# One token per partition in the q/k loads, a quarter of `w_in` ahead, and constants set later, in a chunk-selected attention with a squared-ReLU MLP

## The chip, the cores and the metric

The kernel runs on one core of one Trainium2 chip. The metric is the device time of an execution, in microseconds (us). The kernel before spread over 337.4 to 341.1 us from run to run, and its median over 338.4 to 339.5 us from call to call, so differences below about 1 us between runs of different calls are not read.

## The reference

Attention over 4 batches, 8 heads, 768 tokens and 64 dimensions, in which each query sees only the 6 key chunks (of 32 keys) with the highest upper bound, followed by an MLP with squared ReLU on all 3072 tokens:

```python
k_chunks = k.reshape(B, H, nc, 32, D)                       # nc = 24 chunks
k_min, k_max = k_chunks.min(3), k_chunks.max(3)
ub = sum_d(max(q * k_min, q * k_max))                       # per query and chunk
ub = where(causal_by_chunk, ub, -1e9)
top_chunks = argsort(ub)[..., -6:]
scores = q @ k.T / sqrt(D), masked to top_chunks and to causal positions
attn = softmax(scores) @ v
x = attn.transpose(0, 2, 1, 3).reshape(3072, 512)
h = maximum(x @ w_in, 0)                                    # 512 -> 2048
out = (h * h) @ w_out                                       # 2048 -> 512
```

## The kernel before

The heads go in pairs, and the 768 tokens of a sequence in two halves ("blocks") of 384. `stage_a` prepares a pair: it transposes k and q on TensorE, forms the chunk minima and maxima, the bounds and the selection. `stage_b` makes the scores, exponentials and weighted values of one pair and block, and writes x transposed (`xT`). When all four pairs of a block are done, its MLP units join a list that later `stage_b` calls work off between their own matmuls. The first block of batch 0 has no finished block's MLP beside it, and only six `w_in` matmuls of its own MLP units run in it: I call it the *first stage*, and its end is the last `xT` of pair 3. Pairs are counted from 0, as in the code.

The loads of batches 0 and 1 put three neighbouring tokens on one partition, 384 B of bf16 in one piece. After the transpose the columns are therefore in a permuted order, and copies restore it:

```python
WIDE = (0, 1)
def load_qk(b, h0, h1, halves=(0, 1), what="kq"):
    ...                                                     # [cut]
        if b not in WIDE:     # "h (j p) d -> p (h j) d": one token per partition
            ...
        elif len(halves) == 2:
            nc.gpsimd.dma_start(
                out=dst[:, h0:h1].rearrange("p h t x -> p (h t) x"),
                in_=src[b, h0:h1].rearrange(
                    "h (t p j) d -> p (h t) (j d)", t=2, j=HT))
        else: ...             # the same for one half
```

```python
# stage_a, for k; pt holds the transposed tile in PSUM
if b in WIDE:
    kt = work.tile([128, QB * nt], BF16, tag="kt", name="kt")
    nc.vector.tensor_copy(kt.rearrange("d (t p j) -> d t p j", t=nt, j=HT), by_token)
    flat = kt
...                           # chunk max and min from flat -> kr
for hh in range(2):
    nc.vector.tensor_copy(kbd[s][rows, :, hh, 12 * n0:12 * n1], kr[rows])
    nc.vector.tensor_copy(kq[s][hh][0:D, cols], flat[rows])
# for q
for hh in range(2):
    if b in WIDE:
        nc.scalar.copy(qs[s][hh]..., by_token[rows])             # permuting, on ACT
        src, dst = qs[s][hh][0:D, u0:u0 + m], rows               # then from SBUF
    else: ...                                                    # straight from PSUM
    nc.vector.tensor_scalar_max(qp[dst, 0:m], src, 0.0)
    nc.vector.tensor_scalar_min(qm[dst, 0:m], src, 0.0)
```

The constants, `w_in` and the order of the pieces:

```python
def set_constants(s):
    nc.vector.memset(kbd[s], 0.0)
    for hh in range(2):
        nc.vector.memset(qs[s][hh][D:KC, 0:128], 0.0)
    nc.vector.memset(selb[s], 0.0)
    ...                                                          # [cut]
set_constants(0)
nc.vector.memset(vo[0][:, :, :, D:], 1.0)     # the ones beside v
set_constants(1)
...                                                              # [cut]
put(0, 1, L(load_qk, 0, 0, H, (1,)), L(load_w_in))   # the whole of w_in, 2 MB
put(0, 2, L(load_v, 0, 1))
...                                                              # [cut]
put(1, 0, L(load_qk, 1, 0, H), L(load_w_out), L(load_v, 1))
phases[0][1:1] = [L(set_constants, 2), L(set_constants, 3)]
for ss in range(NP, NSET):
    put(0, ss % NP, L(set_constants, ss))
put(1, 2, L(nc.vector.memset, vo[1][:, :, :, D:], 1.0))
```

`put(ph, i, x)` puts x into the text of the program ahead of pair i in block `ph` (counted over the batches).

The softmax here doesn't subtract the row's maximum and nothing guards it: scores larger than these inputs give would overflow.

Of the kernel before, what the change touches and what calls it, by code (L numbers as in the profile page):

```python
# [10 lines left out]
BF16 = mybir.dt.bfloat16  # L11
AX = mybir.AxisListType
ALU = mybir.AluOpType
ACT = mybir.ActivationFunctionType
# [4 lines left out]
def kernel(  # L19
# [9 lines left out]
    nc = tc.nc  # L29

    B, H, S, D = q.shape
    CH = 32
# [32 lines left out]
    WIDE = (0, 1)  # L65

    def load_qk(b, h0, h1, halves=(0, 1), what="kq"):


        for nm, src in (("k", k), ("q", q)):  # L70
            if nm not in what:
                continue
            if (nm, b) not in nat:
                nat[nm, b] = ld.tile([128, H, 2, HT * D], BF16, tag=nm + "n",
                                     name=nm + "n")
            dst = nat[nm, b]
            if b not in WIDE:
                nc.gpsimd.dma_start(
                    out=dst[:, h0:h1].rearrange(
                        "p h t (j d) -> p (h t j) d", d=D),  # L80
                    in_=src[b, h0:h1].rearrange(
                        "h (j p) d -> p (h j) d", p=128))
            elif len(halves) == 2:
                nc.gpsimd.dma_start(
                    out=dst[:, h0:h1].rearrange("p h t x -> p (h t) x"),
                    in_=src[b, h0:h1].rearrange(
                        "h (t p j) d -> p (h t) (j d)", t=2, j=HT))
            else:
                t = halves[0]
                nc.gpsimd.dma_start(  # L90
                    out=dst[:, h0:h1, t],
                    in_=src[b, h0:h1, QB * t:QB * t + QB].rearrange(
                        "h (p j) d -> p h (j d)", j=HT))
# [35 lines left out]
    def set_constants(s):  # L129
# [3 lines left out]
        nc.vector.memset(selb[s], 0.0)  # L133
# [10 lines left out]
    nc.vector.memset(vo[0][:, :, :, D:], 1.0)  # L144
    set_constants(1)

# [12 lines left out]
    load_v(0, 0)  # L159
# [4 lines left out]
    def load_w_in():  # L164
        nc.gpsimd.dma_start(
            out=w_in_sb, in_=moe_w_in.rearrange("(ki p) f -> p ki f", p=128))
# [5 lines left out]
    def stage_a(p, halves):  # L172
# [10 lines left out]
        for nm in ("k", "q"):  # L183
            pt = pool.tile([128, nt, HT, 128], BF16, tag=tag, name=nm + "T")
            n = nat[nm, b].rearrange("p h t (j d) -> p h t j d", d=D)
            for t in range(nt):
                for j in range(HT):
                    for hh in range(2):
                        nc.tensor.matmul(  # L189
                            pt[D * hh:D * hh + D, t, j],  # L190
                            lhsT=n[:, 2 * hp + hh, n0 + t, j], rhs=ident,
                            is_transpose=True, start=True, stop=True)
            flat = pt.rearrange("d t j p -> d (t j p)")
            by_token = pt.rearrange("d t j p -> d t p j")
            if nm == "k":
                if b in WIDE:
                    kt = work.tile([128, QB * nt], BF16, tag="kt", name="kt")
                    nc.vector.tensor_copy(  # L198
                        kt.rearrange("d (t p j) -> d t p j", t=nt, j=HT),
                        by_token)  # L200
                    flat = kt
                kr = work.tile([128, 2, NC // 2 * nt], BF16, tag="kr",
                               name="kr")
                for mm, op in ((0, ALU.max), (1, ALU.min)):
                    nc.vector.tensor_reduce(  # L205
                        kr[:, mm], flat.rearrange("d (c j) -> d c j", j=CH),
                        axis=AX.X, op=op)
                for hh in range(2):
                    rows = slice(D * hh, D * hh + D)
                    nc.vector.tensor_copy(  # L210
                        kbd[s][rows, :, hh, 12 * n0:12 * n1], kr[rows])
                    nc.vector.tensor_copy(kq[s][hh][0:D, cols], flat[rows])  # L212
                yield
                continue
            qp = work.tile([128, S], BF16, tag="qp", name="qp")
            qm = work.tile([128, S], BF16, tag="qm", name="qm")
            for hh in range(2):
                rows = slice(D * hh, D * hh + D)
                if b in WIDE:
                    nc.scalar.copy(  # L220
                        qs[s][hh][0:D, cols].rearrange(
                            "d (t p j) -> d t p j", t=nt, j=HT),
                        by_token[rows])
                    src, dst = qs[s][hh][0:D, u0:u0 + m], rows
                else:
                    nc.vector.tensor_copy(qs[s][hh][0:D, cols], flat[rows])  # L226
                    if hh == 0:
                        continue
                    src, dst = flat[:, u0 - QB * n0:], slice(0, 128)
                nc.vector.tensor_scalar_max(qp[dst, 0:m], src, 0.0)  # L230
                nc.vector.tensor_scalar_min(qm[dst, 0:m], src, 0.0)  # L231
# [195 lines left out]
    put(0, 1, L(load_qk, 0, 0, H, (1,)), L(load_w_in))  # L427
# [15 lines left out]
    for ss in range(NP, NSET):  # L443
        put(0, ss % NP, L(set_constants, ss))
    put(1, 2, L(nc.vector.memset, vo[1][:, :, :, D:], 1.0))
# [50 lines left out]
```

## Time and profile before

| | before |
|---|---|
| time, median of 3 runs | 338.78 us (338.65 to 339.1) |
| span of the profile | 337.1 us |
| end of the first stage (last `xT` of pair 3) | 48.4 us |
| TensorE (PE) idle in the whole span | 42 us |

The page's line of busy times, and its line of PE in 40 equal slices (each digit is tenths busy, 9 is 90% or more, a slice is 8.4 us):

```profile
PE 295.1 (88%) x2096; PEld 159.0 (47%) x2096; DVE 219.4 (65%) x678; ACT 227.9 (68%) x562; POOL 90.4 (27%) x226
...
PE   1564759989999799999999999999999999999995
```

PE is the limit from about the seventh slice on. What can be won is its idle time at the start. The table of stretches, cut at the ends of the first stage and of later blocks, gives each engine's busy time in each:

```profile
core 0: us, PE busy (x) PEld busy (x) DVE busy (x) ACT busy (x) POOL busy (x), PEclk, DMA share, GB/s
0.00:48.40 48.40, 23.68 (x147) 11.61 (x148) 37.43 (x137) 20.51 (x48) 25.23 (x52) 1.00 1.16 145
48.40:101.60 53.20, 48.90 (x393) 25.62 (x392) 45.92 (x152) 41.10 (x99) 16.67 (x35) 1.00 1.02 94
101.60:174.80 73.20, 69.30 (x544) 38.38 (x543) 55.67 (x166) 53.47 (x134) 20.57 (x48) 1.00 0.50 50
...
```

In the first stage VectorE (DVE) is the busiest, 37.4 of 48.4 us; PE is busy for half of it. PE's waits in the first 50 us (total, times, longest):

```profile
PE ub L243 <- DVE qp L230: 7.6, 3, 5.2
PE ph L302 <- DMA w_in_sb<-in_moe_w_in_dram: 5.2, 1, 5.2
PE kT L189 <- DMA kn<-in_k_dram: 4.3, 1, 4.3
PE sT L263 <- DVE selb L255: 3.5, 3, 1.7
```

The chain that ended last runs through both large stops (start, length, what):

```profile
2.12 2.62 DVE vo L144
...
19.32 15.74 DMA w_in_sb<-in_moe_w_in_dram
35.11 0.82 PE ph L302 x2
```

So DVE set the ones of `vo[0]` before any key was touched, and PE's queue stood behind the first `w_in` matmul until 35.1 us. DVE's timeline around 30 us shows the second set of ones, of `vo[1]`, right ahead of the step of pair 3's selection that PE waits for (`selb`). It is the fourth selection of the stage; the prediction and three of the expectations call it pair 2's.

```profile
29.99 2.62 DVE L424 MEMSET vo<- 128x3072 bf16 x1 [0.59 <-PE av_507 L359]
32.52 0.20 DVE L255 TENSOR_TENSOR selb<-ubm,m_466 128x96 bf16<-128x96 f32 x1
...
36.18 0.60 DVE L268 COPY qsc<-sT 24x256 bf16<-24x256 bf16 x2 [3.01 <-PE sT L263]
```

Some of the costs of DVE in the first stage, by group (busy us, mean ns):

```profile
L212 DVE COPY kqc<-kt 64x384 bf16<-64x384 bf16 x10 | 4.8, 483 | 0.1
...
L144 DVE MEMSET vo<- 128x3072 bf16 x1 | 2.6, 2618 | 0.6 <-issue 0.6
L424 DVE MEMSET vo<- 128x3072 bf16 x1 | 2.6, 2618 | 0.6 <-PE av_507 L359 0.6
```

A `kqc` copy takes 0.25 us when nothing disturbs it. The timelines of DVE and of GpSimd (POOL) show why one of them took 2.03 us: it lay beside the issue of a DMA by POOL.

```profile
42.84 2.03 DVE L212 COPY kqc<-kt 64x384 bf16<-64x384 bf16 x1
```

```profile
42.57 2.21 POOL L102 DMA_DIRECT2D vo<-in_v_dram  x1
```

### The profile page before, as it was taken

How to read it: one execution, taken by the hardware profiler on the slowest of the kernel's cores; microseconds unless marked ns; L12 is line 12 of the kernel's file. 1: busy time of each engine (PE TensorE's matmuls, PEld its weight loads, DVE VectorE, ACT ScalarE, POOL GpSimd, SP SyncE). 2: the span in 40 equal slices, each digit the busy share in tenths (PEclk: the TensorE clock that was granted, in tenths of full speed). 3: DMA queues.
4: the chain of work that ended last, by engine and by line, in shares of the span. 5: the costliest groups of instructions: out<-in, count | busy, mean ns of one | idle time of the engine just before them, and what ended most of it. 6: DMA issues, size and time to landing. Idle time of an engine off the chain costs nothing.

```text
span 337.1 us, 6126 instructions
## 1 busy us (share of the span) xinstructions
PE 295.1 (88%) x2096; PEld 159.0 (47%) x2096; DVE 219.4 (65%) x678; ACT 227.9 (68%) x562; POOL 90.4 (27%) x226
## 2 busy tenths in 40 slices
PE   1564759989999799999999999999999999999995
PEld 0231324544445454555455555555455555554542
DVE  7988488899889948899177467997384413431420
ACT  3363537989568875877658775888469769983731
POOL 8265431362144430221143221112122212220000
PEclk9999999999999999999999999999999999999999
DMA  7979999799059990000039000000110010001001
GB/s 79 174 106 197 142 188 193 53 94 95 33 63 97 126 91 33 32 2 3 31 50 108 0 33 32 33 2 2 48 48 0 3 62 31 2 0 63 33 31 62
DMA packets 64298, 20.86 MB, mean 62 GB/s; under 512 B 58276, under 2 KB 60684, under 8 KB 64268
## 3 DMA queue, kind: packets, MB, share of 16 engines
q0 software_dynamic: 60272, 13.63, 44.8%
q1 hardware_dynamic: 3996, 6.85, 5.4%
q8 instruction: 16, 0.26, 0.3%
q14 instruction: 14, 0.11, 0.1%
HBM read 27.26 MB, written 6.29 MB: 100 GB/s over the span
## 4 chain that ended last, share of the span: by engine, by line
PE 53%; DVE 29%; ACT 9%; DMA 5%; issue 4%; POOL 1%; ACTq 0%; POOLq 0%
PE py L316 20%; PE ph L302 15%; PE ps L393 6%; DMA w_in_sb<-in_moe_w_in_dram 5%; DVE kr L205 5%; DVE xT L383 4%; ACT rc L373 3%; DVE qp L230 3%; DVE kqc L212 2%; DVE qsc L226 2%; ACT e L397 2%; DVE kt L198 2%; PE sT L263 2%; PE kT L189 2%; DVE qm L231 2%
## 5 line engine op out<-in xcount | busy, mean ns | idle before, releaser
L397 ACT ACTIVATE e<-ps 128x384 bf16<-128x384 f32 (+2 forms) x288 | 111.1, 429 | 35.4 <-PE ps L393 34.0
L302 PE MATMUL ph<-xT,w_in_sb 128*128 128x384 bf16 x512 | 106.9, 330 | 8.9 <-DMA w_in_sb<-in_moe_w_in_dram 5.2
L400 POOL TENSOR_SCALAR_AFFINE_SELECT e<-e 128x128 bf16<-128x128 bf16 x192 | 58.5, 311 | 201.5 <-ACT e L397 199.6
L393 PE MATMUL ps<-qsc,kqc 88*128 88x384 bf16 (+2 forms) x288 | 73.2, 305 | 6.4 <-ACT e L397 4.1
L307 ACT ACTIVATE ht<-ph 128x384 bf16<-128x384 f32 x128 | 63.5, 502 | 16.8 <-PE ph L302 15.8
L302 PEld LDWEIGHTS <-w_in_sb 128*128 128x128 bf16 x512 | 48.5, 98 | 43.0 <-issue 12.2
L393 PEld LDWEIGHTS <-kqc 88*128 88x128 bf16 x288 | 27.5, 100 | 21.9 <-issue 5.4
L359 PEld LDWEIGHTS <-vo 128*128 128x128 bf16 x288 | 27.8, 101 | 19.2 <-issue 2.2
L321 ACT COPY ob<-py 128x512 f32<-128x512 f32 x24 | 14.1, 587 | 19.3 <-PE py L316 19.1
L205 DVE TENSOR_REDUCE kr<-kT 128x24 bf16<-128x768 bf16 x16 | 14.6, 952 | 15.9 <-PE kT L189 15.9
L220 ACT COPY qsc<-qT 64x384 bf16<-64x384 bf16 (+1 forms) x24 | 13.9, 580 | 11.4 <-PE qT L189 11.0
L268 DVE COPY qsc<-sT 24x640 bf16<-24x640 bf16 (+2 forms) x40 | 16.7, 417 | 6.5 <-PE sT L263 5.8
L243 PE MATMUL ub<-kbd,qp 128*128 128x48 bf16 x80 | 8.8, 190 | 11.3 <-DVE qp L230 9.9
L376 ACT ACTIVATE rc<-rc 128x384 f32<-128x384 f32 x32 | 16.5, 515 | 0.1
L205 DVE TENSOR_REDUCE kr<-kt 128x12 bf16<-128x384 bf16 (+1 forms) x24 | 15.5, 677 | 0.2
L189 PE MATMUL kT<-ident,kn 128*64 128x128 bf16 x192 | 11.0, 240 | 4.9 <-DMA kn<-in_k_dram 4.3
L243 PEld LDWEIGHTS <-qp 128*128 128x128 bf16 x80 | 5.8, 98 | 17.2 <-DVE qp L230 13.2
L189 PEld LDWEIGHTS <-kn 128*64 128x64 bf16 x192 | 7.0, 116 | 12.6 <-DMA kn<-in_k_dram 4.3
L263 PE MATMUL sT<-ident,selb 128*128 128x128 bf16 x80 | 8.5, 232 | 4.6 <-DVE selb L255 4.5
L189 PE MATMUL qT<-ident,qn 128*64 128x128 bf16 x192 | 11.0, 240 | 0.9 <-DMA qn<-in_q_dram 0.7
L198 DVE COPY kt<-kT 128x384 bf16<-128x384 bf16 (+1 forms) x12 | 8.3, 691 | 4.7 <-PE kT L189 4.5
L189 PEld LDWEIGHTS <-qn 128*64 128x64 bf16 x192 | 7.1, 117 | 8.6 <-issue 4.7
(653 smaller groups left out, 522.5 us busy)
## 6 DMA issues: line engine op xcount, KB each, us to landing
out_dram<-ob SPq DMA_DIRECT2D x24, 256.0 KB
kn<-in_k_dram POOLq DMA_DIRECT2D x3, 768.0 KB, 9.3
qn<-in_q_dram POOLq DMA_DIRECT2D x3, 768.0 KB, 9.2
vo<-in_v_dram POOLq DMA_DIRECT2D x3, 768.0 KB, 10.2
w_in_sb<-in_moe_w_in_dram POOLq DMA_DIRECT2D x1, 2048.0 KB, 15.7
w_out_sb<-in_moe_w_out_dram POOLq DMA_DIRECT2D x1, 2048.0 KB, 16.1
vo<-in_v_dram POOLq DMA_DIRECT2D x6, 128.0 KB, 8.6
kqc<-kqc SPq DMA_DIRECT2D x15, 36.0 KB
```

Source lines behind the costliest of these rows:

```text
L189: nc.tensor.matmul(pt[D * hh:D * hh + D, t, j], lhsT=n[:, 2 * hp + hh, n0 + t, j], rhs=ident, is_transpose=True, start=True, stop=True)
L205: nc.vector.tensor_reduce(kr[:, mm], flat.rearrange("d (c j) -> d c j", j=CH), axis=AX.X, op=op)
L263: nc.tensor.matmul(sT[:, 128 * i:128 * (i + 1)], lhsT=selb[s][:, u0 - 1 + i:u0 + 1 + i], rhs=ident, is_transpose=True, start=(i == 0), sto ...
L268: nc.vector.tensor_copy(qs[s][hh][D:KC, 128 * u0:128 * t1], sT[32 * hh:32 * hh + NC, :])
L302: nc.tensor.matmul(ph, lhsT=w_in_sb[:, ki, 128 * f:128 * (f + 1)], rhs=xT[:, ki], start=(ki == 0), stop=(ki == NKI - 1))
L307: nc.scalar.activation(ht, ph, ACT.Relu)
L316: nc.tensor.matmul(py, lhsT=h2[f][:, 128 * t:128 * (t + 1)], rhs=w_out_sb[:, f, :], start=(f == 0), stop=(f == NFI - 1))
L359: nc.tensor.matmul(hold["av"][hh][:, off:], lhsT=vo[b % 2].rearrange("p h n d -> p (h n d)")[:, c0:c0 + 2 * D], rhs=es[hh][:, off:], start ...
L376: nc.scalar.activation(rc, rc, ACT.Exp, scale=-1.0)
L393: nc.tensor.matmul(ps[:, off:], lhsT=kq[s][hh][:, 128 * j:128 * (j + 1)], rhs=qs[s][hh][:, q0 + off:q1], start=True, stop=True)
L397: nc.scalar.activation(e[:, off:], ps[:, off:], ACT.Exp, scale=scale)
L400: nc.gpsimd.affine_select(out=e[:, off:off + 128], in_=e[:, off:off + 128], compare_op=ALU.is_ge, fill=0.0, base=0, channel_multiplier=-1, ...
```

## The change

The intent is to shorten the first stage. The change has three parts:

- **Part L, the loads.** Every q/k load puts one token on one partition (packets of 128 B written instead of 384 B). The permuting copies go: k's `kt` copy on DVE and q's copies on ACT. q is copied by DVE, and `kqc`, `qp` and `qm` are made straight from PSUM.
- **Part W, `w_in`.** A quarter of its columns is loaded ahead of the second half of the sequence.
- **Part C, the constants.** The ones of `vo[0]` go to ACT, the zeros of `selb` shrink, and sets 4 to 7 and the ones of `vo[1]` (in six pieces) are written into the program's second block.

```diff
 # part L
-            if b not in WIDE: ...                      # [cut: three forms of load]
+            if j1 - j0 == NT:                          # both halves: one DMA
+                ... src[b, h0:h1].rearrange("h (j p) d -> p (h j) d", p=128)
+            if h1 - h0 <= j1 - j0:                     # few heads: a DMA per head
+                ...
+            for j in range(j0, j1):                    # else a DMA per 128 tokens
+                nc.gpsimd.dma_start(
+                    out=nat[nm, b][:, h0:h1, j],
+                    in_=src[b, h0:h1, 128 * j:128 * (j + 1)].rearrange("h p d -> p h d"))
 # [cut: the transposes, the same matmuls into a plain [128, nt * QB] tile]
+            for hh in range(2):
+                rows = slice(D * hh, D * hh + D)
+                nc.vector.tensor_copy(ops[s][hh][0:D, cols], pt[rows])   # k and q
             if nm == "k":
-                if b in WIDE: kt = ...; nc.vector.tensor_copy(kt..., by_token)
-                    nc.vector.tensor_copy(kq[s][hh][0:D, cols], flat[rows])
-            for hh in range(2): ...                    # [cut: q on ACT; qp, qm by halves]
+        nc.vector.tensor_scalar_max(qp[:, 0:m], pt[:, u0 - QB * n0:], 0.0)
+        nc.vector.tensor_scalar_min(qm[:, 0:m], pt[:, u0 - QB * n0:], 0.0)
 # part W
-    put(0, 1, L(load_qk, 0, 0, H, (1,)), L(load_w_in))
+    load_w_in(0, 4)                                    # after load_v(0, 0)
+    put(0, 1, L(load_qk, 0, 0, H, (1,)), L(load_w_in, 4, NFI))
 # part C
-        nc.vector.memset(selb[s], 0.0)
+        nc.vector.memset(selb[s][:, :, :, NC:], 0.0)
+        nc.vector.memset(selb[s][:, NT - 1], 0.0)
-    nc.vector.memset(vo[0][:, :, :, D:], 1.0)
+    for j in range(2):
+        nc.scalar.activation(vo[0][:, :, HT * j:HT * (j + 1), D:],
+            ident[:, 0:1]...to_broadcast([128, H, HT, D]), ACT.Copy, scale=0.0, bias=1.0)
-        put(0, ss % NP, L(set_constants, ss))
-    put(1, 2, L(nc.vector.memset, vo[1][:, :, :, D:], 1.0))
+        put(1, 1, L(set_constants, ss))
+    for j in range(NT):
+        put(1, j // 2 + 1, L(nc.vector.memset, vo[1][:, :, j, D:], 1.0))
```

More of the change, by code (lines that the diff above doesn't have):

```diff
@@ L63 @@
     nat = {}
-    WIDE = (0, 1)
     def load_qk(b, h0, h1, halves=(0, 1), what="kq"):
@@ L73, in load_qk @@
             if (nm, b) not in nat:
-                nat[nm, b] = ld.tile([128, H, 2, HT * D], BF16, tag=nm + "n",
+                nat[nm, b] = ld.tile([128, H, NT, D], BF16, tag=nm + "n",
                                      name=nm + "n")
-            dst = nat[nm, b]
-            if b not in WIDE:
+            j0, j1 = HT * halves[0], HT * (halves[-1] + 1)
+            if j1 - j0 == NT:
                 nc.gpsimd.dma_start(
-                    out=dst[:, h0:h1].rearrange(
-                        "p h t (j d) -> p (h t j) d", d=D),
-                    in_=src[b, h0:h1].rearrange(
-                        "h (j p) d -> p (h j) d", p=128))
-            elif len(halves) == 2:
-                nc.gpsimd.dma_start(
-                    out=dst[:, h0:h1].rearrange("p h t x -> p (h t) x"),
-                    in_=src[b, h0:h1].rearrange(
-                        "h (t p j) d -> p (h t) (j d)", t=2, j=HT))
-            else:
-                t = halves[0]
-                nc.gpsimd.dma_start(
-                    out=dst[:, h0:h1, t],
-                    in_=src[b, h0:h1, QB * t:QB * t + QB].rearrange(
-                        "h (p j) d -> p h (j d)", j=HT))
+                    out=nat[nm, b][:, h0:h1].rearrange("p h j d -> p (h j) d"),
+                    in_=src[b, h0:h1].rearrange("h (j p) d -> p (h j) d",
+                                                p=128))
+                continue
+            if h1 - h0 <= j1 - j0:
+                for h in range(h0, h1):
+                    nc.gpsimd.dma_start(
+                        out=nat[nm, b][:, h, j0:j1],
+                        in_=src[b, h, 128 * j0:128 * j1].rearrange(
+                            "(j p) d -> p j d", p=128))
+                continue
+            for j in range(j0, j1):
+                nc.gpsimd.dma_start(
+                    out=nat[nm, b][:, h0:h1, j],
+                    in_=src[b, h0:h1, 128 * j:128 * (j + 1)].rearrange(
+                        "h p d -> p h d"))
     vo = [consts.tile([128, H, NT, 2 * D], BF16, tag=f"vo{s}", name="vo")
@@ L143 @@
     set_constants(0)
-    nc.vector.memset(vo[0][:, :, :, D:], 1.0)
     set_constants(1)
+    for j in range(2):
+        nc.scalar.activation(
+            vo[0][:, :, HT * j:HT * (j + 1), D:],
+            ident[:, 0:1].unsqueeze(2).unsqueeze(3).to_broadcast(
+                [128, H, HT, D]), ACT.Copy, scale=0.0, bias=1.0)
     ubmask = consts.tile([128, NS, 1, NC], F32, tag="ubmask")
@@ L158, with load_w_in @@
         )
-    load_v(0, 0)
     w_in_sb = consts.tile([128, NKI, d_ff], BF16, tag="w_in_sb")
     w_out_sb = consts.tile([128, NFI, d_model], BF16, tag="w_out_sb")
-    def load_w_in():
+    def load_w_in(f0, f1):
+        cols = slice(128 * f0, 128 * f1)
         nc.gpsimd.dma_start(
-            out=w_in_sb, in_=moe_w_in.rearrange("(ki p) f -> p ki f", p=128))
+            out=w_in_sb[:, :, cols],
+            in_=moe_w_in[:, cols].rearrange("(ki p) f -> p ki f", p=128))
+    load_v(0, 0)
+    load_w_in(0, 4)
     def load_w_out():
@@ L183, in stage_a @@
         for nm in ("k", "q"):
-            pt = pool.tile([128, nt, HT, 128], BF16, tag=tag, name=nm + "T")
-            n = nat[nm, b].rearrange("p h t (j d) -> p h t j d", d=D)
-            for t in range(nt):
-                for j in range(HT):
-                    for hh in range(2):
-                        nc.tensor.matmul(
-                            pt[D * hh:D * hh + D, t, j],
-                            lhsT=n[:, 2 * hp + hh, n0 + t, j], rhs=ident,
-                            is_transpose=True, start=True, stop=True)
-            flat = pt.rearrange("d t j p -> d (t j p)")
-            by_token = pt.rearrange("d t j p -> d t p j")
-            if nm == "k":
-                if b in WIDE:
-                    kt = work.tile([128, QB * nt], BF16, tag="kt", name="kt")
-                    nc.vector.tensor_copy(
-                        kt.rearrange("d (t p j) -> d t p j", t=nt, j=HT),
-                        by_token)
-                    flat = kt
+            pt = pool.tile([128, nt * QB], BF16, tag=tag, name=nm + "T")
+            for j in range(nt * HT):
+                for hh in range(2):
+                    nc.tensor.matmul(
+                        pt[D * hh:D * hh + D, 128 * j:128 * (j + 1)],
+                        lhsT=nat[nm, b][:, 2 * hp + hh, n0 * HT + j], rhs=ident,
+                        is_transpose=True, start=True, stop=True)
+            ops = kq if nm == "k" else qs
+            for hh in range(2):
+                rows = slice(D * hh, D * hh + D)
+                nc.vector.tensor_copy(ops[s][hh][0:D, cols], pt[rows])
+            if nm == "k":
                 kr = work.tile([128, 2, NC // 2 * nt], BF16, tag="kr",
@@ L205, in stage_a @@
                     nc.vector.tensor_reduce(
-                        kr[:, mm], flat.rearrange("d (c j) -> d c j", j=CH),
+                        kr[:, mm], pt.rearrange("d (c j) -> d c j", j=CH),
                         axis=AX.X, op=op)
@@ L211, in stage_a @@
                         kbd[s][rows, :, hh, 12 * n0:12 * n1], kr[rows])
-                    nc.vector.tensor_copy(kq[s][hh][0:D, cols], flat[rows])
                 yield
-                continue
-            qp = work.tile([128, S], BF16, tag="qp", name="qp")
-            qm = work.tile([128, S], BF16, tag="qm", name="qm")
-            for hh in range(2):
-                rows = slice(D * hh, D * hh + D)
-                if b in WIDE:
-                    nc.scalar.copy(
-                        qs[s][hh][0:D, cols].rearrange(
-                            "d (t p j) -> d t p j", t=nt, j=HT),
-                        by_token[rows])
-                    src, dst = qs[s][hh][0:D, u0:u0 + m], rows
-                else:
-                    nc.vector.tensor_copy(qs[s][hh][0:D, cols], flat[rows])
-                    if hh == 0:
-                        continue
-                    src, dst = flat[:, u0 - QB * n0:], slice(0, 128)
-                nc.vector.tensor_scalar_max(qp[dst, 0:m], src, 0.0)
-                nc.vector.tensor_scalar_min(qm[dst, 0:m], src, 0.0)
+        qp = work.tile([128, S], BF16, tag="qp", name="qp")
+        qm = work.tile([128, S], BF16, tag="qm", name="qm")
+        nc.vector.tensor_scalar_max(qp[:, 0:m], pt[:, u0 - QB * n0:], 0.0)
+        nc.vector.tensor_scalar_min(qm[:, 0:m], pt[:, u0 - QB * n0:], 0.0)
         yield
```

## The prediction

> **What bounds the kernel now.** The page gives PE 295.1 of 337.1 us busy (88%), ACT 68%, DVE 65%. The table of stretches shows where PE's 42 idle us lie: it is busy 25 us of the first 50, 72.7 of 79 us from 49 to 128, and about 96% from 128 to 280. So only the opening, the four head pairs of the first half sequence, has much to give. There the limit is DVE, busy 38.5 of 50 us, with two stops shown by the chain of waits and the timeline:
> - DVE spends 2.62 us (2.12 to 4.74) setting the ones of vo, then about 3 us on other constants, before it touches the first kT at 7.75, though PE had transposed it by 4.8.
> - PE idles from 29.9 to 35.1: pair 2's selection stood behind the second vo memset (2.62 us, until 32.6), and then PE's queue stood behind the first w_in matmul, whose whole-tensor load took 15.7 us to land (5.2 us in the list of waits). Dense matmuls start only at about 49 us. Until then a 384-column matmul takes 0.53 us instead of 0.325.
>
> **What the change does, with durations from the trace.**
> - DVE up to 49 us. Removed: both vo memsets (5.2), five permuting kt copies (0.56 each, 2.8), about 2.5 of memsets of sets 4 to 7, and qp/qm as half-partition pairs (-1.6). Added: eight q copies from PSUM at an estimated 0.35 (as the 24x384 PSUM copies) = 2.8, and 0.1 more for each k copy = 0.8. Net about -8 us. The ones of vo[0] go to ACT, idle then.
> - ACT loses 24 q copies (13.9 us), mostly where it is no limit.
> - PE's wait for w_in goes: a quarter is enough for the first four units and should land at about 20 us.
> - DVE in the second stage (49 to 95): kt copies off (-4.6), q and k copies on (+6.9), qp/qm -1.9, and moved here vo[1] (+3.3) and sets 4 to 7 (+2.5): about +6 us on an engine busy 39 of 46 us. I expect 2 to 3 us back.
> - DMA. The q/k packets of batches 0 and 1 go from 8192 of 384 B written to 24576 of 128 B. The Trainium skill, "DMA: Bandwidth & Descriptors", Specifications, asks for at least 512 B for line rate; the trace agrees mildly: 128 B packets ran at 156 GB/s (70 to 74 us), 1 KB ones at 202 (47 to 52). Half a q/k load costs about 1.5 us more.
> - POOL issues more DMAs (0.77 to 0.9 each): estimated +11 us in the first 50, where it is busy 25. So pair 1's q lands 2 to 3 us later, and selects of e can stand behind issues. The skill's "SBUF — State Buffer", "SBUF: two separate sides", says that DVE and GpSimd can block each other; here a kqc copy took 2.03 us instead of 0.25 during a 2.21 us issue.
>
> **Sum.** First stage ends about 10 us earlier (DVE -8, w_in stop and idle DVE -3, later q +1 to 2), 2 to 3 us returned in the second: net -8. **330.5 us**, range 325 to 336.5. Chances: faster 0.60, same 0.35, slower 0.05.
>
> **What would show it.** First kT-derived DVE work at about 5.5 us; no idle PE of 5 us before the first w_in matmul; dense matmuls from about 39 us; DVE over 90% in the stage after; the last 200 us unchanged.
>
> **What would make it wrong.** The opening bound by POOL's issues or the late q of pair 1 (gain under 4 us); the second stage DVE-bound and returning most of it; the rest of w_in or v's second half landing after its first use.

## The result, and the profile after

| | before | after |
|---|---|---|
| time, median of 4 runs each | 338.94 us (338.65 to 341.06) | 330.22 us (329.88 to 330.36) |
| ratio, after to before | | 0.9728 (95%: 0.9688 to 0.9768) |
| span of the profile | 337.1 us | 328.7 us |
| end of the first stage | 48.4 us | 41.6 us |
| first copy out of a kT by DVE | 7.75 us | 7.97 us |
| first bounds matmul (`ub`) | 11.15 us | 12.08 us |
| first scores matmul (`ps`) | 15.31 us | 16.32 us |
| first `w_in` matmul | 35.11 us | 27.73 us |

Ratios here and below are the mean time of one kernel's runs over the mean of the other's of the same rounds, so they are not quite the ratio of the medians quoted. The first column is the kernel before as run beside the change, so its median is not quite that of the section above. All outputs are right.

The page after, the same two lines (a slice is 8.2 us). 20 matmul records of PE are missing from this trace, as its weight loads still number 2096:

```profile
PE 294.6 (90%) x2076; PEld 158.7 (48%) x2096; DVE 219.1 (67%) x678; ACT 218.2 (66%) x540; POOL 99.1 (30%) x237
...
PE   1397699999998999999999999999999999999995
```

PE's busy time did not change; its idle time went from 42.0 to 34.1 us, and most of that (6.6 us) in the first 50 us, where PE was busy 25.19 us before and 31.83 after. The table of stretches, cut at the same four events (columns as before):

```profile
0.00:41.60 41.60, 23.70 (x144) 11.57 (x145) 34.98 (x138) 18.54 (x40) 34.22 (x62) 1.00 1.44 135
41.60:88.50 46.90, 44.72 (x334) 23.34 (x339) 37.85 (x123) 33.04 (x85) 17.25 (x34) 1.00 1.53 129
88.50:167.50 79.00, 73.50 (x597) 40.32 (x601) 66.42 (x196) 53.89 (x135) 20.12 (x50) 1.00 0.53 51
...
```

Three readings:

1. The first stage is 6.8 us shorter. DVE is busy 2.5 us less in it (37.43 to 34.98) and idle 4.4 us less (48.40 − 37.43 = 11.0, against 41.60 − 34.98 = 6.6). The opening itself gained nothing: the first scores of pairs 0, 1 and 2 began at 15.3, 20.6 and 25.5 us before and at 16.3, 21.5 and 26.5 after. From pair 2's to pair 3's it took 11.0 us before and 5.0 after, which is 6.0 of the gain, and from there to the end of the stage 11.9 and 10.2.
2. The second and third rows can only be compared as a sum, because MLP units moved between them: 126.4 us before, 125.9 after, with 118.2 us of PE work in both. So the second stage gave nothing back that can be seen.
3. The rest, from there to the end of the span, is 1.1 us shorter (162.3 and 161.2 us). The lead over before, measured at each block's last `xT`, is 7.3 us at 167.5 and 7.8 to 8.2 from then on. That last part is at the limit of what the runs resolve.

PE's waits in the first 50 us:

```profile
PE kT L194 <- POOL ident masks.py:199: 4.3, 1, 4.3
PE kT L194 <- DVE kr L206: 3.3, 2, 2.6
```

There is no wait for `w_in` any more. The 4.3 us at the very start is the same wait as before under another name: such a wait is put down to whichever of its releasers came last. The quarter of `w_in` was issued at 14.08 us and landed 8.4 us later, 5 us ahead of the first matmul that reads it:

```profile
27.73 0.52 PE L288 MATMUL ph<-xT,w_in_sb 128*128 128x384 bf16 x1
```

DVE's timeline, at the start and at pair 3's selection:

```profile
5.27 0.48 DVE L410 MEMSET vo<- 128x512 bf16 x1
...
5.85 2.11 DVE L410 MEMSET vo<- 128x512 bf16 x4
7.97 0.72 DVE L201 COPY kqc<-kT 64x384 bf16<-64x384 bf16 x2
...
29.94 0.28 DVE L241 TENSOR_TENSOR selb<-ubm,m_454 128x96 bf16<-128x96 f32 x1
30.99 0.60 DVE L254 COPY qsc<-sT 24x256 bf16<-24x256 bf16 x2 [0.77 <-PE sT L249]
```

Pair 3's selection (the prediction and three of the expectations call it pair 2's) is no longer cut in two, and its result is copied at 30.99 instead of 36.18. But the ones of `vo[1]`, which the source has in the second block, ran at 5.27 to 7.97, ahead of the first work on a key: five of the six pieces there and the sixth at 9.78. The zeros of sets 4 to 7 ran there too. The compiled program had moved both forward. DVE's groups in the first stage that answer to those of before:

```profile
L201 DVE COPY qsc<-qT 64x384 bf16<-64x384 bf16 x10 | 3.5, 353 | 0.2
L201 DVE COPY kqc<-kT 64x384 bf16<-64x384 bf16 x10 | 3.5, 352 | 0.2
L410 DVE MEMSET vo<- 128x512 bf16 x6 | 2.9, 485 | 0.3
```

The `kqc` copy reads PSUM now, which costs 0.35 us instead of the undisturbed 0.25, and yet the group became cheaper: 3.5 instead of 4.8 us. The timelines of DVE and POOL at the long issues show the reason. Only a copy from SBUF (`kbd<-kr`) is stretched; the copies from PSUM, and `qp` and `qm`, ran at their normal length beside two issues:

```profile
35.22 1.78 DVE L211 COPY kbd<-kr 64x24 bf16<-64x24 bf16 x2
...
38.20 0.72 DVE L201 COPY qsc<-qT 64x384 bf16<-64x384 bf16 x2
...
39.21 0.35 DVE L217 TENSOR_SCALAR qm<-qT 128x384 bf16<-128x384 bf16 x1
```

```profile
34.62 2.23 POOL L75 DMA_DIRECT2D kn<-in_k_dram  x1
36.84 2.23 POOL L75 DMA_DIRECT2D qn<-in_q_dram  x1
39.04 1.18 POOL L176 DMA_DIRECT2D w_out_sb<-in_moe_w_out_dram  x1
```

This fits two pages of the Trainium skill taken together. "SBUF — State Buffer", "Who interferes with whom", says that a DVE instruction in a two-port mode and a GpSimd instruction block each other, and that one with at most one SBUF input outside those modes does not. "VectorE: DVE Perf Modes", "Why PSUM operands drop a tier", says that an operand in PSUM rules the two-port mode out. The traces agree in one more respect: over the first 130 us of before, after and all runs below, every DVE operation held for more than 0.4 us beside an issue read SBUF, and ended between 0.04 us before and 0.16 us after the end of the issue (one exception, 0.59 us after, in `late_q_on_act`).

To put a number on it I use one measure throughout, the **collision loss**: for each DVE instruction that lay beside a DMA issue by POOL, its duration above the lower quartile of all instructions of the same line and shapes, where that excess is over 0.1 us, summed over the first 130 us. It was 4.9 us before and 2.9 us after.

### The profile page after: what moved, and what is told of

Read it like the earlier page. It is cut to its first block, busy times and chain, and to the rows that moved or that the text cites. A ratio compares the mean times of both kernels' runs of the same rounds, so it can differ in the third digit from the quotient of the medians.

```text
span 328.7 us, 6090 instructions
## 1 busy us (share of the span) xinstructions
PE 294.6 (90%) x2076; PEld 158.7 (48%) x2096; DVE 219.1 (67%) x678; ACT 218.2 (66%) x540; POOL 99.1 (30%) x237
## 4 chain that ended last, share of the span: by engine, by line
PE 55%; DVE 24%; ACT 8%; DMA 6%; issue 3%; POOL 2%; ACTq 0%; DVEq 0%
PE py L302 21%; PE ph L288 13%; PE ps L379 8%; DMA w_out_sb<-in_moe_w_out_dram 6%; DVE kr L206 4%; ACT rc L359 4%; DVE xT L369 3%; DVE qsc L201 3%; ACT e L383 2%; DVE kqc L201 2%; PE sT L249 2%; DVE qsc L254 1%; ACT rc L362 1%; PE kT L194 1%; DVE qp L216 1%
## 5 line engine op out<-in xcount | busy, mean ns | idle before, releaser
L383 ACT ACTIVATE e<-ps 128x384 bf16<-128x384 f32 (+2 forms) x288 | 108.6, 430 | 37.1 <-PE ps L379 34.6
L386 POOL TENSOR_SCALAR_AFFINE_SELECT e<-e 128x128 bf16<-128x128 bf16 x192 | 55.9, 302 | 183.4 <-ACT e L383 181.6
L288 PE MATMUL ph<-xT,w_in_sb 128*128 128x384 bf16 x512 | 105.3, 331 | 4.8 <-ACT ht L293 3.0
L379 PE MATMUL ps<-qsc,kqc 88*128 88x384 bf16 (+2 forms) x288 | 72.2, 303 | 6.2 <-ACT e L383 2.8
L307 ACT COPY ob<-py 128x512 f32<-128x512 f32 x24 | 14.2, 590 | 25.7 <-PE py L302 25.5
L206 DVE TENSOR_REDUCE kr<-kT 128x24 bf16<-128x768 bf16 (+1 forms) x40 | 30.3, 793 | 0.3
L201 DVE COPY kqc<-kT 64x768 bf16<-64x768 bf16 (+1 forms) x40 | 18.9, 474 | 16.9 <-PE kT L194 16.3
L201 DVE COPY qsc<-qT 64x768 bf16<-64x768 bf16 (+1 forms) x40 | 18.9, 473 | 1.2 <-PE qT L194 0.6
L194 PEld LDWEIGHTS <-kn 128*64 128x64 bf16 x192 | 6.8, 116 | 16.3 <-issue 6.5
L229 PE MATMUL ub<-kbd,qp 128*128 128x48 bf16 x80 | 7.7, 190 | 3.4 <-DVE qm L217 2.1
L211 DVE COPY kbd<-kr 64x48 bf16<-64x48 bf16 (+1 forms) x40 | 10.0, 251 | 0.5
L234 DVE TENSOR_TENSOR ubm<-ub,ubmask 128x240 f32<-128x240 f32 (+2 forms) x20 | 7.1, 353 | 4.5 <-PE ub L231 4.3
## 6 DMA issues: line engine op xcount, KB each, us to landing
vo<-in_v_dram POOLq DMA_DIRECT2D x3, 768.0 KB, 10.2
w_in_sb<-in_moe_w_in_dram POOLq DMA_DIRECT2D x1, 1536.0 KB, 11.7
```

The lines of the kernel that those rows point to most:

```text
L194: nc.tensor.matmul(pt[D * hh:D * hh + D, 128 * j:128 * (j + 1)], lhsT=nat[nm, b][:, 2 * hp + hh, n0 * HT + j], rhs=ident, is_transpose=Tru ...
L201: nc.vector.tensor_copy(ops[s][hh][0:D, cols], pt[rows])
L206: nc.vector.tensor_reduce(kr[:, mm], pt.rearrange("d (c j) -> d c j", j=CH), axis=AX.X, op=op)
L288: nc.tensor.matmul(ph, lhsT=w_in_sb[:, ki, 128 * f:128 * (f + 1)], rhs=xT[:, ki], start=(ki == 0), stop=(ki == NKI - 1))
L379: nc.tensor.matmul(ps[:, off:], lhsT=kq[s][hh][:, 128 * j:128 * (j + 1)], rhs=qs[s][hh][:, q0 + off:q1], start=True, stop=True)
L383: nc.scalar.activation(e[:, off:], ps[:, off:], ACT.Exp, scale=scale)
```

## The experiments

**The theories.** Two questions were open.

*Why did the first stage gain 6.8 us and not 10?* Theory: DVE limits it, and the constants that moved ahead of the first key cost what is missing. Rival: POOL's issues and the later arrival of q and k pace it, so that DVE time given back there is not gained.

*What is part L worth, when it trades one set of copies for another?* Theory: its worth is that DVE reads PSUM and is no longer held up beside POOL's issues. Rival: it is the saved copy time on DVE and ACT alone, and collisions don't matter.

### First call: each part alone, and the moved ones taken out

`w_only` is before with part W:

```diff
+    load_v(0, 0)
+    load_w_in(0, 4)
-    put(0, 1, L(load_qk, 0, 0, H, (1,)), L(load_w_in))
+    put(0, 1, L(load_qk, 0, 0, H, (1,)), L(load_w_in, 4, NFI))
```

> Kernel before with one part of the change: a quarter of w_in loaded ahead, the rest later. Sum theory (three causes, each worth a few us): PE's 5.2 us stop at the first w_in matmul goes, but pair 2's selection still stands behind the second vo memset until 32.6, so only about 2 to 3 us come off: 336 to 337. Rival (the early w_in quarter is the whole gain): 330 to 331.5, with dense matmuls from about 41.

Measured: 336.4 us (335.8 to 337.21), ratio 0.9913 (0.9875 to 0.995), end of the first stage 45.8 us, first `w_in` matmul at 26.89. Pair 3's first scores came at 33.8 us instead of 36.5, PE having waited 2.9 us for the selection behind the second set of ones.

`loads_only` is before with part L:

```diff
-    WIDE = (0, 1)
+    # loads, transposes, copies, qp and qm as in part L of the change   [cut]
```

> Kernel before with one part of the change: one token per partition, no permuting copies. Sum theory: DVE's total hardly changes, the w_in load still lands at about 35 or later behind three times the packets, so between no gain and 2 us: 337 to 339. Rival (the permuting copies and their two-step chain through ACT were the limit): 332 to 333.

Measured: 335.12 us (334.3 to 335.63), ratio 0.9871 (0.9835 to 0.9908), end of the first stage 47.7 us. The first stage gained only 0.7, since PE still stood 5.8 us for `w_in`; the other 3 us came in the later blocks. The collision loss fell to 0.95 us from the 4.9 of before.

`consts_only` is before with part C:

```diff
-    nc.vector.memset(vo[0][:, :, :, D:], 1.0)
+    # the ones of vo[0] on ACT, smaller zeros of selb, sets 4 to 7 and
+    # the ones of vo[1] written in block 1, as in part C               [cut]
```

> Kernel before with one part of the change: constants set otherwise (vo[0] on ACT, vo[1] in six pieces, sets 4 to 7 later, smaller selb memsets). The compiled order puts all of these memsets before the first kt copy, so the opening does not get shorter; pair 2's selection is freed (second vo memset gone from 30 to 32.6), but PE still waits for w_in at about 35. Sum theory: 0 to 2 us off, 337 to 339. Rival (constants on DVE are the limit of the opening): 333 to 335.

Measured: 334.24 us (333.39 to 335.55), ratio 0.9851 (0.9809 to 0.9893), end of the first stage 44.1 us. By the medians it is the largest of the single parts (its interval overlaps that of `loads_only`), although it removes only one of the two sets of ones from the first stage: the time from pair 2's to pair 3's first scores fell from 11.0 to 5.7 us. PE's wait for `w_in` fell to 1.5 us with no change to that load, which landed 1.2 us earlier (33.8); three of pair 3's score matmuls now ran ahead of the wait.

`late_ones` is after with the ones of `vo[1]` made from a loaded tile, so that they cannot run before batch 1's k has landed:

```diff
+    def ones_late(j):
+        nc.vector.tensor_scalar(
+            out=vo[1][:, :, j, D:], in0=nat["k", 1][:, :, j, :],
+            scalar1=0.0, scalar2=1.0, op0=ALU.mult, op1=ALU.add)
-        put(1, j // 2 + 1, L(nc.vector.memset, vo[1][:, :, j, D:], 1.0))
+        put(1, j // 2 + 1, L(ones_late, j))
```

> Kernel after, with the ones of vo[1] made from batch 1's k rows (times 0 plus 1), so that the scheduler cannot put them ahead of the first kT work. If the opening is bound by DVE as predicted, the first k copy starts at about 5.8 instead of 7.97 and the gain reaches the end: about 328. Rival (after that the loads' arrival paces pairs 1 and 2): no change, 330 to 330.5.

Measured: 329.95 us (329.77 to 330.73), ratio 0.9728 (0.9687 to 0.9769), the same ratio as after; end of the first stage 41.3 us against 41.6. Its DVE timeline:

```profile
5.43 0.72 DVE L201 COPY kqc<-kT 64x384 bf16<-64x384 bf16 x2
...
11.32 0.72 DVE L201 COPY kqc<-kT 64x384 bf16<-64x384 bf16 x2 [2.38 <-PE kT L194]
```

The first key was touched 2.5 us earlier (5.43 for 7.97), close to the 5.5 that had been predicted for the change, and the first bounds came 1.9 us earlier (10.22 for 12.08). But then DVE stood 2.38 us for pair 1's kT, and the first scores came only 0.7 us earlier (15.58 for 16.32). So the constants that moved ahead do explain the late opening, and they do not explain the missing time: without them the time went into a wait. Here the rival is right.

### Second call: each part left out, and the loads in pairs

`no_consts` is parts W and L, `no_loads` is W and C, `no_w_in` is L and C: after, with one part as in before.

```diff
# no_consts, against after
-    for j in range(2):
-        nc.scalar.activation(vo[0][:, :, HT * j:HT * (j + 1), D:], ...)
+    nc.vector.memset(vo[0][:, :, :, D:], 1.0)
-        put(1, 1, L(set_constants, ss))
+        put(0, ss % NP, L(set_constants, ss))
     # [cut: the other lines of part C]
# no_loads, against after
+    WIDE = (0, 1)
     # [cut: loads, copies, qp and qm as in before]
# no_w_in, against after
-    load_w_in(0, 4)
-    put(0, 1, L(load_qk, 0, 0, H, (1,)), L(load_w_in, 4, NFI))
+    put(0, 1, L(load_qk, 0, 0, H, (1,)), L(load_w_in))
```

> Kernel after without the constants' part (so w_in quarter and loads alone). The single parts took off 2.5, 3.8 and 4.7 us (w_in, loads, constants); if they add, this is about 332.5 to 333. Since the part was found to set all constants before the first k work either way, the worth of it must lie at pair 2, where the second vo memset stood: first k work on DVE at about 7.8 as in the kernels before and after. Rival (constants matter for the opening): first k work later than 8.5.

> Kernel after without the loads' part (w_in quarter and constants, wide loads and permuting copies as before). If the parts add: about 331.7 to 332.5. Rival (the loads' part is a loss once the other two are there, since its packets are three times as many and POOL issues 11 more DMAs): 330 or less.

> Kernel after without the w_in quarter (loads and constants alone). If the parts add: about 331.5 to 332.5. Rival (interaction: the loads' part delays w_in, which landed at 36.5 with it alone, so the freed DVE time is lost in PE's queue behind the first w_in matmul): 333.5 or more, with a wait of several us for w_in.

With the first call, this is the whole table of eight combinations (median of runs, ratio, end of the first stage, collision loss to 130 us):

| parts | run | time, us | ratio (95%) | first stage ends | collision loss |
|---|---|---|---|---|---|
| none | before | 338.94 | 1 | 48.4 | 4.9 |
| W | w_only | 336.40 | 0.9913 (0.9875–0.995) | 45.8 | 5.4 |
| L | loads_only | 335.12 | 0.9871 (0.9835–0.9908) | 47.7 | 0.95 |
| C | consts_only | 334.24 | 0.9851 (0.9809–0.9893) | 44.1 | 3.6 |
| W, C | no_loads | 336.15 | 0.9927 (0.9882–0.9971) | 45.8 | 7.6 |
| W, L | no_consts | 332.77 | 0.9830 (0.9786–0.9873) | 44.5 | 0.8 |
| L, C | no_w_in | 333.22 | 0.9837 (0.9784–0.9889) | 45.4 | 1.5 |
| W, L, C | after | 330.22 | 0.9728 (0.9688–0.9768) | 41.6 | 2.9 |

The median of before in the second call was 338.39 us. The parts don't add up. Alone they gain 2.5, 3.8 and 4.7 us, 11.0 together, and the change gained 8.7. The odd one is W with C, which gains less (2.2 us against before of its own call) than C alone (4.7); by the ratios 0.7% against 1.5%. Without W, PE stands for `w_in` again, as the waits of `no_w_in` say:

```profile
PE ph L284 <- DMA w_in_sb<-in_moe_w_in_dram: 4.3, 1, 4.3
```

What goes wrong in `no_loads` can be read from its DVE and POOL timelines at the end of the first stage. `kqc`, `qp` and `qm` read SBUF there, and those of pair 0's second half (384 columns of q), which are made before the last `xT` of the stage, fall beside a row of DMA issues:

```profile
36.45 0.90 DVE L221 COPY kqc<-kt 64x384 bf16<-64x384 bf16 x1
...
38.72 2.00 DVE L240 TENSOR_SCALAR qm<-qsc 64x384 bf16<-64x384 bf16 x1
```

```profile
36.12 1.16 POOL L84 DMA_DIRECT2D qn<-in_q_dram  x1
...
38.40 2.25 POOL L102 DMA_DIRECT2D vo<-in_v_dram  x1
```

Each of those takes about 0.25 us undisturbed (the copy and the `qm` alike). Between 30 and 50 us the loss was 3.7 us. That W, which made the stage earlier, brought this work onto the issues is so far only a reading; it is tested in the third call.

`late_pairwise` tests the rival of the first question: `late_ones`, with k and q of pairs 1 to 3 loaded pair by pair, both halves at once, so that pair 1's comes first:

```diff
-    load_qk(0, 2, H, (0,))
+    for h in range(2, H, 2):
+        load_qk(0, h, h + 2)
-    put(0, 1, L(load_qk, 0, 0, H, (1,)), L(load_w_in, 4, NFI))
+    put(0, 1, L(load_qk, 0, 0, 2, (1,)), L(load_w_in, 4, NFI))
```

> Kernel after with late ones, and with the k and q of pairs 1 to 3 of batch 0 loaded whole, pair by pair (6 DMAs instead of 6 by token tile and 6 for the second half). With late ones alone DVE waited 2.4 us for pair 1's kT, and later for q, behind POOL's issues. If the arrival of pair 1 is the limit of the opening: pair 1's kT at about 9, first stage 1.5 to 2.5 us shorter, 327.5 to 328.5. Rival (the chain of DVE, PE and ACT within a pair is): within 0.5 us of 330.

Measured: 332.38 us (331.97 to 332.47), ratio 0.9816 (0.9772 to 0.9859), slower than `late_ones`; end of the first stage 43.1 us against 41.3. Pair 1's kT was made earlier, at 9.51 us. But the loads now carried second halves that nobody needed yet. Pair 0's bounds were done by 10.7 us, and DVE's next step on them (`ubm`) ran only at 16.65, behind copies of pairs 1 and 2 whose transposes waited for data (PE's timeline):

```profile
12.42 0.53 PE L195 MATMUL qT<-ident,qn 128*64 128x128 bf16 x6 [1.75 <-DMA qn<-in_q_dram]
...
19.25 0.50 PE L380 MATMUL ps<-qsc,kqc 88*128 88x384 bf16 x1
```

They started at 19.25 us instead of 15.58. So the order in which the loads arrive does move the first stage, here for the worse, by way of the order of work on DVE. A loading order that is better than that of after was not found.

### Third call: the issues moved, and `qp`/`qm` put back to SBUF

`no_loads_later_issue` takes `no_loads` and moves only the place of the issues of batch 1's q, k and v: one pair later, and so behind that of `w_out`.

```diff
-    put(1, 0, L(load_qk, 1, 0, H), L(load_w_out), L(load_v, 1))
+    put(1, 0, L(load_w_out))
+    put(1, 1, L(load_qk, 1, 0, H), L(load_v, 1))
```

> The kernel without the loads' part, with batch 1's k, q and v loads issued one head pair later and w_out first. In that kernel four SBUF-to-SBUF operations of DVE took 0.8 to 2.0 us instead of 0.25 beside POOL's DMA issues at 35 to 40.6 us, 3.7 us lost on the chain of the first stage. Collision theory (the loads' part is worth 6 us mostly because its copies read PSUM and do not meet POOL): the loss in 30 to 50 us falls below 1 us, the first stage ends at 42.5 to 44 instead of 45.8, time 332.5 to 334.5. Rival (the permuting copies and the detour of q through ACT are what cost): 335.5 to 336.5.

Measured: 333.03 us (332.64 to 333.77), ratio 0.9804 (0.9774 to 0.9834) against 0.9927 for `no_loads`; end of the first stage 42.7 us against 45.8. The loss between 30 and 50 us fell from 3.7 to 1.29 us. No computing instruction was changed. In its trace the two DVE lines that were shown for `no_loads` in the second call read:

```profile
36.45 0.26 DVE L221 COPY kqc<-kt 64x384 bf16<-64x384 bf16 x1
...
37.35 0.25 DVE L240 TENSOR_SCALAR qm<-qsc 64x384 bf16<-64x384 bf16 x1
```

From 26 us up to this copy DVE's timelines of the two runs agree to about 0.1 us. From here three operations took 0.26, 0.25 and 0.25 us instead of 0.90, 0.97 and 2.00, and the `xT` behind them came at 37.62 instead of 40.75. These 3.1 us are the whole gain of the stage, so the rivals that the move also touches (POOL's own selects behind the issues, the earlier landing of `w_out`) have no share in it; `w_out` isn't read in it at all.

`after_later_issue` is the same edit on after:

> Kernel after, with batch 1's k, q and v loads issued one head pair later and w_out first. In the kernel after one kbd copy (SBUF to SBUF) took 1.6 instead of 0.17 us beside such an issue at 35.2, and the first py waited for w_out at 60.1. Collision theory: about 1 us less, 329 to 329.5. Rival (off the chain): 330 to 330.4.

Measured: 331.37 us (330.87 to 332.52), ratio 0.9757 (0.9724 to 0.979), which is no better than after. The first stage ended 0.8 us earlier (40.8), but the second block ended later (90.3 against 88.5), and the collision only moved: a `kbd` copy took 1.91 us at 48.23. A side effect that I had not counted on: `w_out`, now issued first, landed in 14.6 us instead of 21.0. In after, PE had waited only 0.4 us for it.

The pair of runs decides the second question. The same move of the issues gained 3.1 us by the medians (4.2 by the ratios, as before was 1.1 us slower in this call) where DVE reads SBUF, and nothing where it reads PSUM. That is a good half of the 5.9 us (6.7 by the ratios) by which `no_loads` is slower than after. So the theory holds for that part of it, and the odd pair of the table is explained: with the issues moved, W and C together (0.9804) are no longer behind C alone (0.9851). The rest may be the copies themselves or collisions that remain (4.2 us of loss in `no_loads_later_issue`, against 2.9 in after); that is not separated.

`qp_from_sbuf` is after with `qp` and `qm` made from the copied q in SBUF, by halves of the partitions, in all batches:

```diff
-        nc.vector.tensor_scalar_max(qp[:, 0:m], pt[:, u0 - QB * n0:], 0.0)
-        nc.vector.tensor_scalar_min(qm[:, 0:m], pt[:, u0 - QB * n0:], 0.0)
+        for hh in range(2):
+            rows = slice(D * hh, D * hh + D)
+            src = qs[s][hh][0:D, u0:u0 + m]
+            nc.vector.tensor_scalar_max(qp[rows, 0:m], src, 0.0)
+            nc.vector.tensor_scalar_min(qm[rows, 0:m], src, 0.0)
```

> Kernel after, with qp and qm made from the q rows in SBUF as the kernel before did (four half-partition operations) instead of from PSUM. By the durations this adds about 0.3 us of DVE work for each of 24 units, some 5 us up to the end of the second stage. Collision theory: on top of it these operations are stretched beside POOL's issues, 2 us or more more lost than the 2.9 of the kernel after, and the time is 332.5 or more. Rival (only the work counts, and DVE has room): 330 to 331.5.

Measured: 337.63 us (337.39 to 337.79), ratio 0.9934 (0.9901 to 0.9968), 7.4 us more than after; end of the first stage 42.8 us. DVE was busy 225.8 us instead of 219.1, and the collision loss was 5.8 instead of 2.9 us. The run mixes two things, as the four half operations cost more by themselves (25.6 us for all `qp` and `qm`, with their stretching, instead of 16.8). It says that where `qp` and `qm` are read from matters much; how much of it is collision it can't say.

### Fourth call: less DVE work in the first stage

`late_q_on_act` gives the q copies of the first stage to ACT:

```diff
# against late_ones
-                nc.vector.tensor_copy(ops[s][hh][0:D, cols], pt[rows])
+                copy = (nc.scalar.copy if nm == "q" and p < NP and n1 == 1
+                        else nc.vector.tensor_copy)
+                copy(ops[s][hh][0:D, cols], pt[rows])
```

> Kernel with late ones, and with the q copies of batch 0's first half on ACT instead of DVE (8 copies of 0.36 us, 2.9 us of DVE work; 0.47 each on ACT, which was busy 13.8 of the first 30 us at most). So far the time moved nearly one to one with DVE's busy time wherever it was not waiting for loads (2.8 us less gave 3.1, 6.7 more gave 7.4). If that holds: first stage ends 1.5 to 3 us earlier than 41.3, time 327 to 328.5. Rival (pairs 1 to 3 of the first stage are paced by loads and by the PE-ACT-POOL chain): 329.7 to 330.3; or worse, if q stands behind e in ACT's queue.

Measured over 5 rounds: 332.01 us (331.57 to 332.12), ratio 0.9794 (0.9766 to 0.9822). DVE was busy 215.8 us instead of the 218.0 of `late_ones`, and the kernel was 2 us slower; the first stage ended at 42.3 us against 41.3. DVE now waited 6.2 us for kT in the first 45 us. That the first stage gives back DVE time one to one falls with this run. It does not show that DVE no longer matters there: pair 3's first scores came 1.9 us earlier than in `late_ones` (28.85 for 30.74). But then the six value matmuls (`av`) of pair 1 ran between pair 3's first and second score matmul, the last two score matmuls waited for ACT, and when the value matmuls of pair 2 began, at 33.76 us (33.69 in `late_ones`), the lead was gone. DVE then did the next q copies before pair 2's `xT`, which PE waited 1.27 us for (37.08 for 36.26). So the order of work, on PE and DVE, took the gain back. The rest of the 2 us was lost in the second block, which I did not trace.

## Why the prediction was right

The time, 330.22 us for 330.5, the direction and the stage in which the gain lies were right. The sum behind it was 10 us in the first stage less 2 to 3 in the second. The runs show 6.8 in the first, nothing given back, and about 1 us later on. So two terms were wrong in opposite directions, and part of the closeness is luck.

- **"DVE −8" in the first stage: wrong.** It was −2.5. The term that failed is the constants: both sets of ones and sets 4 to 7, −7.7 us, were taken as gone from this stage. All DVE memsets in it summed to 9.6 us before and 7.0 after, so −2.6: the six pieces of `vo[1]` (2.9 us) and sets 4 to 7 (2.0 us) stayed in it and ran ahead of the first key. The trace of before had the warning in it. There too, the zeros of sets 4 and 5, written ahead of pairs 0 and 1 and after the first pair's `stage_a`, ran between 6.5 and 7.7 us, before the first key was touched.
- **"First kT-derived DVE work at about 5.5 us": wrong**, 7.97, for the same reason. `late_ones` gave 5.43.
- **Where the gain lies: mostly at the second of the two stops that it names.** Up to pair 2's first scores the kernel is 0.9 us later than before. The 6.0 us between pair 2's and pair 3's come from freeing pair 3's selection from the second set of ones and PE from the wait for `w_in`: the stretch of 11.0 us took 8.2 in `w_only`, 5.7 in `consts_only`, 10.7 in `loads_only` and 5.0 with all three.
- **What a microsecond of DVE is worth: overrated.** `late_ones` won 2.5 us at the start and 0.3 at the end of the first stage; `late_q_on_act` relieved DVE further and was slower. The list of what could go wrong did name an opening bound by POOL's issues, with a gain under 4 us; `late_ones`' wait of 2.38 us for pair 1's kT, whose transposes waited for k, is of that kind; the gain was 6.8.
- **"w_in stop and idle DVE −3": right in kind, too small.** DVE's idle time fell by 4.4 us and PE's wait of 5.2 us for `w_in` is gone. The quarter landed at about 22.5 us for a predicted 20. `no_w_in`, which lacks only this, is 3.0 us slower than after (3.7 by the ratios).
- **"2 to 3 us returned in the second stage": wrong.** The expected DVE load of over 90% was 81% (37.85 of 46.9 us), since the memsets weren't there, and the second and third stretches together took 125.9 us for 126.4. In `late_ones`, where the ones of `vo[1]` do run in the second block (44.0 to 50.9 us), it took 46.5 us against 46.9 in after, so there was room for that work.
- **POOL's issues: right.** Predicted +11 us in the first 50; measured +12.8 (POOL busy 25.23 to 37.98), of which +11.7 are the issues (16.9 to 28.5). The last transpose of pair 1's q began 1.2 us later (13.21 for 12.05), where 2 to 3 was predicted.
- **Smaller packets: borne out in kind.** In the first 50 us the share of the DMA engines' time taken rose from 1.16 to 1.64, while the rate fell from 147 to 140 GB/s. That agrees in kind with the 512 B which the Trainium skill, "DMA: Bandwidth & Descriptors", Specifications, gives as the smallest transfer for line rate; 128 and 384 B both lie below it, so the figure itself was not tested.
- **"Dense matmuls from about 39 us": late.** The first MLP activation ran at 42.1 us (before: 49.0), the gain being 6.8 and not 10.
- **"The last 200 us unchanged": right**, to about 1 us.
- **Not foreseen:** the prediction saw a copy stretched to 2.03 us beside an issue and counted it only as a risk of more issues. It costed `kqc` copies from PSUM at +0.8 us, and they came out 1.3 us cheaper than before (4.8 to 3.5). It did not see that part L takes most DVE work out of POOL's way, which the two runs with moved issues show to be worth about 3 us to the other parts.

Left open: what exactly paces pairs 1 to 3 after the change, the loads or the chain from PE over ACT to POOL; and where about 1 us of lead after the third stretch comes from. Of all versions run none is clearly faster than after: `late_ones` has the same ratio.

## What to carry to other kernels

A memset has no input, so the place where it is written doesn't hold it there: look in the trace of the kernel at hand where such instructions really run, and give one a true dependence if it has to wait. When a resource has been relieved, ask what the next wait is before crediting the relief one to one: here 2.5 us less before the first key became a 2.4 us wait for the next. On a core whose GpSimd issues the DMAs, an SBUF-to-SBUF copy on VectorE that is faster by itself can be the slower one, so its mean in the trace counts and not its best, and moving an issue by one pair can be worth as much as removing work (3.1 us in `no_loads`, nothing in after).

## What the Trainium skill lacked or had wrong

- "SBUF — State Buffer", "Who interferes with whom", and "VectorE: DVE Perf Modes", "Why PSUM operands drop a tier": both rules agree with the traces, but neither page draws the consequence that a DVE copy or `tensor_scalar` that reads PSUM gets out of the way of DMA issues by GpSimd, nor how long an issue can hold one (the first has only a ratio, "DVE 6.8× slower"). Here operations of 0.25 us took up to 2.0 us when they read SBUF beside a 2.2 us issue, and 0.35 us when they read PSUM. Moving the issues gained 3.1 us in one kernel.
- "DMA: Bandwidth & Descriptors", "Anatomy of one DMA — SWDGE (gpsimd) path": it gives about 50 ns for the sequencer's dispatch and calls descriptor generation small and variable (elsewhere the page puts the first byte at about 1 us). Here one issue kept GpSimd busy for 0.77 us (a quarter of `w_in`) to 2.23 us (q or k of a batch in 128 B packets; 1.16 us in packets of 384 B), and the issues of the first 50 us took 28.5 us of GpSimd together.
- "TensorE: Matmul & The Clock Gate", "Seeing it yourself", says that clock events in the trace have been seen to be unreliable: nothing is wrong there, the traces agree. The record says full clock from the start, while 384-column matmuls took 0.52 us in the first stage and 0.33 us later; in `no_loads` it says half clock for 30 to 50 us with the same 0.53 us.
- No page says that instructions without inputs may run far ahead of where they are written: here the ones of `vo[1]`, written in the second block, ran at 5.27 us.
